# The fold of the last input piece on GpSimd, and its two hidden-transform blocks right behind the routing list

## The chip, the cores and the metric

The kernel runs on one core of a Trainium2 chip. The metric is the device time of one execution in microseconds (us). Five engines work side by side, each through its own instructions in order: TensorE (PE, with its weight loads as PEld), VectorE (DVE), ScalarE (ACT), GpSimd (POOL) and SyncE (SP, which issues DMAs).

## The reference

```
x = A_x                                   # 1 x 2048 x 448, float32
g = sigmoid((x * gate_w).sum(-1))
a = Real(DFT_seq(DFT_hidden(x)))          # both DFTs as products with the given cos and sin matrices
b = mixture of experts on x:              # 8 experts, F = 1792, top 2 of softmax(x @ wg)
      h = gelu(x @ w1[e]);  y = h @ w2[e];  b = sum of the two experts, weighted
out = g * a + (1 - g) * b
```

## The kernel before, in words

The first 40 us or so hold the DFT branch and the routing. The experts, a long chain of matmuls on TensorE, follow.

**The DFT branch.** The input comes in four pieces `c` = 0 to 3 of 512 rows each, tile `xraw` (`XR[c]`), each by two DMAs of 512 KB, one for each half `r`. The symmetries of the DFT are folded in with additions and subtractions: `fold_near` (line 501, `pq` from `xraw`), `fold_half` (505 and 506, `eo` from `pq`), `fold_quarter` (518, `fr` from `eo`). Each instruction here has 512 elements on 128 partitions, or 1024 for `fold_near` where both halves go together, and both inputs lie in SBUF. `pq` and `eo` have two buffers each, so piece 3 uses those of piece 1. A folded piece gives two blocks `v` = 2c and 2c+1. `hidden(v)` (line 527) multiplies `fr` of a block by the hidden DFT's matrix and ACT copies the result to `ab[:, v]` (line 528). `even(m)` then uses blocks 0 to 3 for the sequence DFT (line 466), `odd(m, v)` uses blocks 4 to 7 (line 570).

**The routing**, a generator stepped by `advance()`. The logits of all pieces end in a PSUM tile. DVE picks the two best experts of each token (252 to 265, up to tile `mb`), TensorE counts (269 to 275), and DVE makes two lists `oh` and `ov` (285 to 301), which TensorE joins with 16 small matmuls (309, the routing list's matmuls). From these come `tok0` (313), the rows that the first expert gathers. GpSimd issues these gathers (547, tiles `hi`, `lo`, `up`, `dn`, `xg`), and TensorE transposes each gathered tile (`turn0`, 683).

**Order.** Instructions of PE, DVE, ACT and SP run in the order in which the code is written (a manual schedule). GpSimd's queue is left to the scheduler. In the kernel before, GpSimd does constants in the first 4.4 us and then nothing until the first gather. Piece 3 is folded by DVE behind the routing list: half of `fold_near` before the first gather is issued, the rest behind `upper(0)` and `upper(1)`, which are ACT's preparation of the first expert weights. `hidden(6)` and `hidden(7)` follow all of `odd` for blocks 4 and 5, and `odd` for blocks 6 and 7 comes last.

Of the kernel before, what the change touches and what calls it, by code (L numbers as in the profile page):

```python
# [15 lines left out]
OP = mybir.AluOpType  # L16
# [31 lines left out]
NQT = QT // P  # L48
# [14 lines left out]
def r32(ap):  # L63
    return ap.bitcast(F32)
# [7 lines left out]
def tile_kernel(ctx: ExitStack, tc: tile.TileContext, xt, xrows, xplain, wg, whid, cq, cw, cspec, edge, refs, wquad, whall, cgen, wcat, out):  # L72
    nc = tc.nc
    te, ve, se, gp, sp = nc.tensor, nc.vector, nc.scalar, nc.gpsimd, nc.sync
# [16 lines left out]
    XR = {}  # L91
# [93 lines left out]
    def halves(acc):  # L185
        return acc.rearrange("p (u n) -> p u n", u=2)[:, :, :HE]
# [23 lines left out]
    def upper(k):  # L210
        W[k] = [stream.tile([P, DX], F32R, name=n) for n in ("hi", "lo")]
        V[k] = [stream.tile([P, DX], F32R, name=n, bufs=4) for n in ("up", "dn")]
        for (hi, _), raw in zip((W[k], V[k]), RAW[k]):
            se.activation(hi[:, : raw.shape[-1]], raw, AF.Copy)  # L214
# [255 lines left out]
    def advance(n=1):  # L470
        for _ in range(n):
            next(route, None)
# [4 lines left out]
    FH, LT, PQ, EO = {}, {}, {}, {}  # L477
# [18 lines left out]
    def fold_near(c, *rs):  # L496
        if c not in PQ:
            PQ[c] = hp.tile([P, 2, 2, 2, P], F32, name="pq")
            EO[c] = hp.tile([P, 2, 2, 2, P], F32, name="eo")
        for r in rs:  # L500
            ve.tensor_tensor(PQ[c][:, r], XR[c][:, r, :, 0], XR[c][:, r, :, 1], OP.add)

    def fold_half(c, r):
        raw, pq, eo = XR[c], PQ[c], EO[c]
        ve.tensor_tensor(eo[:, r, 0], pq[:, r, :, 0], pq[:, r, :, 1], OP.add)
        ve.tensor_tensor(eo[:, r, 1], pq[:, r, :, 0], pq[:, r, :, 1], OP.subtract)
        if c == 0:
            if r.start:
                ve.tensor_copy(xs, eo[:, 1, 0, :, 0:1].to_broadcast([P, 2, P]))
                for k in range(2):  # L510
                    ve.tensor_tensor(eo[:, k, 0, :, 0:1], raw[:, 0, :, 0, k, 0:1], raw[:, 0, :, 1, 1 - k, 0:1], OP.add)
                ve.memset(eo[:, 0, 1, :, 0:1], 0.0)

    def fold_quarter(c, *rs):
        if c not in FH:
            FH[c] = hp.tile([P, 2, 2, 2, P], F32, name="fr", bufs=NQT)
        for r in rs:
            ve.tensor_tensor(FH[c][:, r], EO[c][:, 0], EO[c][:, 1], OP.subtract if r else OP.add)

    def hidden(v, between=None):  # L520
        fr = FH[v // 2][:, v % 2]
        acc = ps.tile([P, 512], F32, name="acc")
        for u in range(2):
            if between and u == 1:
                between()
            for c in range(2):
                te.matmul(acc[:, 256 * u + HH * c : 256 * u + HH * (c + 1)], fr[:, u, c], wr[:, u, c], start=True, stop=True)
        se.activation(ab[:, v], halves(acc), AF.Copy)

    def special():  # L530
        acc = ps.tile([P, 512], F32, name="acc")
        for c in range(2):
            te.matmul(acc[:, HH * c : HH * (c + 1)], xs[:, c], wr[:, 0, c], start=True, stop=True)
        se.activation(mid[:, 1], acc[:, :HE], AF.Copy)
# [7 lines left out]
    def gather0(c, n):  # L542
        if c < FULL:
            XG[c] = r32(stream.tile([P, DX], F32R, name=("hi", "lo", "up", "dn")[c], bufs=3 if c < 2 else 4))
        else:
            XG[c] = xp.tile([P, NQ, P], F32, name="xg", bufs=2).rearrange("p q d -> p (q d)")
        gp.indirect_dma_start(out=XG[c][:n], out_offset=None, in_=xplain,
                              in_offset=bass.IndirectOffsetOnAxis(ap=rt["tok0"][:n, c : c + 1], axis=0))
# [34 lines left out]
    for r in range(2):  # L583
        fold_near(0, r)
        fold_half(0, slice(r, r + 1))
    fold_quarter(0, 0, 1)
    logits(0, 0)
    turn_over(3)
# [5 lines left out]
    hidden(0)  # L594
    hidden(1)
    fold_near(1, slice(0, 2))
    fold_half(1, slice(0, 2))
    fold_quarter(1, 0, 1)
    logits(2, 0, 1)
    evacuate(2)  # L600
# [6 lines left out]
    hidden(3)  # L607
    flip(3)
    fold_near(2, slice(0, 2))
    fold_half(2, slice(0, 2))  # L610
    fold_quarter(2, 0)
    se.activation(ch[:, :, 0:1], spec[:, 3:, None], AF.Copy)
    special()
    even(0)
# [7 lines left out]
        fetch(k)  # L622
    even(3)
    hidden(4)
    fold_near(3, 0)
    hidden(5)
    odd(0, 4)
    advance(2)
    for c, n in enumerate(tl0[:FULL]):
        gather0(c, n)  # L630
    advance()
    for v in (4, 5):
        for m in range(v == 4, NQT):
            odd(m, v)
    upper(0)
    upper(1)
    fold_near(3, 1)
    fold_half(3, slice(0, 2))
    fold_quarter(3, 0, 1)
    hidden(6)  # L640
    hidden(7)
    hid_stack.close()

    xp = ctx.enter_context(tc.tile_pool(name="xp", bufs=2))
# [530 lines left out]
    hidden = dram.tile([NT, P, 2 * D], F32, name="hidden")  # L1175
# [140 lines left out]
```

## Time and profile before

| | us |
|---|---|
| median of 3 runs | 633.23 |
| lowest and highest run | 633.11, 633.78 |
| the profiled execution | 633.83 |
| its span, first to last instruction | 632.0 |
| PE busy in the span | 622.2 (98%) |
| DVE busy | 506.0 (80%) |
| ACT busy | 289.3 (46%) |
| POOL busy | 214.7 (34%) |

The profiled execution is 0.60 us over the median, and 1.83 us of it lie outside its span. Busy shares are averages over very different stages: PE is busy nearly everywhere, so a microsecond counts if PE waits in it.

### The profile page before, as it was taken

What the parts mean: (1) busy time and instruction counts of PE and PEld (TensorE: products, weight loads), DVE (VectorE), ACT (ScalarE), POOL (GpSimd) and SP (SyncE); (2) the same over time, 40 slices, a digit from 0 to 9 for tenths busy, and PEclk for the clock granted to TensorE, in tenths of its full rate; (3) what the DMA queues carried; (4) which work ended last, traced back from release to release, by engine and by line L of the source; (5) the groups of instructions that cost most, each with busy time, mean ns of one, the idle gap of its engine ahead of it and who ended that gap; (6) DMA issues with size and microseconds to landing.
All of it is one profiled execution on the core that took longest, in us unless ns stands there. A gap on an engine that the chain in (4) does not pass through costs nothing. (4 is left out here: it accounts for less than half of the span.)

```text
span 632.0 us, 10936 instructions
## 1 busy us (share of the span) xinstructions
PE 622.2 (98%) x3581; PEld 556.6 (88%) x3581; DVE 506.0 (80%) x1262; ACT 289.3 (46%) x588; POOL 214.7 (34%) x198
## 2 busy tenths in 40 slices
PE   9999999999999999999999999999999999999995
PEld 5999999999998999989999788888888888888884
DVE  8889798679977999779896799988997788665561
ACT  2553233555565566564664434333342334544440
POOL 2210074635154353344450444333341342142113
PEclk9999999999999999999999999999999999999998
DMA  8556454597777777776776867879576637768734
GB/s 343 183 155 214 146 192 145 159 257 231 219 223 196 200 241 233 222 185 210 243 236 209 204 187 241 261 195 287 176 220 193 152 119 150 158 157 159 154 68 60
DMA packets 58751, 122.97 MB, mean 195 GB/s; under 512 B 8304, under 2 KB 31920, under 8 KB 58688
## 3 DMA queue, kind: packets, MB, share of 16 engines
q1 hardware_dynamic: 47376, 101.95, 50.0%
q0 software_dynamic: 11168, 20.20, 17.9%
q8 instruction: 30, 0.49, 0.3%
q14 instruction: 33, 0.27, 0.1%
q10 hardware_dynamic: 144, 0.07, 0.0%
HBM read 106.09 MB, written 16.08 MB: 193 GB/s over the span
## 5 line engine op out<-in xcount | busy, mean ns | idle before, releaser
L766 PE MATMUL acc<-X,hi 128*128 128x288 f32 (+3 forms) x1050 | 216.1, 342 | 0.0
L653 POOL DMA_INDIRECT xg<-xrows,piece x115 | 126.3, 1098 | 212.2 <-DVE xq L662 130.9
L766 PEld LDWEIGHTS acc<-X,hi 128*128 128x128 f32 x1050 | 173.8, 188 | 19.6 <-issue 1.4
L826 PE MATMUL y<-up,gh 128*128 128x448 f32 (+1 forms) x458 | 167.4, 366 | 0.0
L826 PE MATMUL y<-dn,gh 128*128 128x448 f32 (+1 forms) x458 | 167.4, 366 | 0.0
L826 PE MATMUL y<-up,gl 128*128 128x448 f32 (+1 forms) x444 | 162.5, 366 | 0.0
L773 ACT ACTIVATE g<-acc 128x288 f32<-128x288 f32 (+3 forms) x126 | 61.8, 491 | 194.6 <-issue 106.5
L766 PE MATMUL acc<-X,lo 128*128 128x288 f32 (+3 forms) x672 | 134.8, 322 | 0.0
L766 PEld LDWEIGHTS acc<-X,lo 128*128 128x128 f32 x672 | 105.6, 188 | 10.2
L889 POOL DMA_INDIRECT out<-ys,tok x36 | 63.8, 1771 | 110.9 <-DVE ys L877 53.3
L826 PEld LDWEIGHTS y<-up,gh 128*128 128x128 f32 (+1 forms) x458 | 85.8, 187 | 7.6
L826 PEld LDWEIGHTS y<-dn,gh 128*128 128x128 f32 (+1 forms) x458 | 85.8, 187 | 7.6
L790 DVE TENSOR_TENSOR gl<-g,gh 128x512 fp32r<-128x512 f32 (+1 forms) x111 | 76.4, 689 | 19.5 <-ACT gh L784 13.3
L930 DVE CUSTOM_DVE_ANT_0 junk<-quads 128x512 f32<-128x512 f32 x128 | 88.0, 687 | 2.2
L826 PEld LDWEIGHTS y<-up,gl 128*128 128x128 f32 (+1 forms) x444 | 83.2, 187 | 7.3 <-DVE gl L790 0.2
L219 DVE TENSOR_TENSOR lo<-raw,hi 128x512 fp32r<-128x512 f32 x112 | 77.0, 687 | 2.0 <-ACT hi L214 1.1
L786 DVE CAST gh<-g 128x512 fp32r<-128x512 f32 (+2 forms) x69 | 30.5, 441 | 57.1 <-ACT g L773 56.8
L214 ACT ACTIVATE hi<-raw 128x512 fp32r<-128x512 f32 x112 | 69.4, 619 | 0.0
L219 DVE TENSOR_TENSOR dn<-row,up 128x448 fp32r<-128x448 f32 x112 | 69.1, 617 | 0.0
L214 ACT ACTIVATE up<-row 128x448 fp32r<-128x448 f32 x112 | 63.3, 565 | 0.4 <-DMA row<-wcat 0.4
L771 ACT ACTIVATE g<-acc 128x256 f32<-128x256 f32 x42 | 16.1, 383 | 48.2 <-PE acc L766 47.9
L773 ACT ACTIVATE g<-g 128x256 f32<-128x256 f32 x42 | 17.6, 418 | 37.4 <-DVE g L772 37.4
(276 smaller groups left out, 435.2 us busy)
## 6 DMA issues: line engine op xcount, KB each, us to landing
quads<-cq SPq DMA_DIRECT2D x64, 512.0 KB, 5.2
raw<-wcat SPq DMA_DIRECT2D x112, 256.0 KB, 2.9
row<-wcat SPq DMA_DIRECT2D x112, 224.0 KB, 3.4
out<-yt SPq DMA_DIRECT2D x21, 224.0 KB, 3.2
xraw<-xt SPq DMA_DIRECT2D x8, 512.0 KB, 6.9
out<-ot POOLq DMA_DIRECT2D x16, 224.0 KB, 4.0
cw<-cw SPq DMA_DIRECT2D x4, 512.0 KB, 9.3
xg<-xrows,piece POOLq DMA_INDIRECT x115, 3.7
```

Of the source, the lines that this page charges most:

```text
L214: se.activation(hi[:, : raw.shape[-1]], raw, AF.Copy)
L219: ve.tensor_tensor(lo[:, :n], raw, r32(hi[:, :n]), OP.subtract)
L653: st = gp.indirect_dma_start(out=xg[:, q], out_offset=None, in_=xrows, in_offset=bass.IndirectOffsetOnAxis(ap=rt["piece"][:, e, g : g + 1] ...
L766: te.matmul(acc[:, :m], a, b, start=s == 0, stop=s == len(steps) - 1)
L771: se.activation(g[:, cs], acc[:, n : 2 * n], AF.Copy)
L773: se.activation(g[:, cs], g[:, cs] if both else acc[:, :n], AF.Gelu_apprx_tanh)
L786: ve.tensor_copy(gh[:, :top], g[:, :top])
L790: ve.tensor_tensor(gl[:, :main], g[:, :main], r32(gh[:, :main]), OP.subtract)
L826: te.matmul(Y[c][:m, :D], a, b, start=f == 0 and s == 0, stop=f == NF - 1 and s == len(steps) - 1)
L889: st = gp.indirect_dma_start(out=out, out_offset=bass.IndirectOffsetOnAxis(ap=rt["tok"][:n, e, c : c + 1], axis=0), in_=ys[:n], in_offset= ...
L930: ve.tensor_tensor_reduce(out=junk[:, :512], in0=row(a[0])[:, a[1] * 512 : a[1] * 512 + 512], in1=row(b[0])[:, b[1] * 512 : b[1] * 512 + 5 ...
```

## The change

Everything is the same but for piece 3. Its six fold instructions run on GpSimd, written right behind the fold of piece 2. `hidden(6)` and `hidden(7)` are written behind the gathers' issue, ahead of `odd` for blocks 4 and 5.

```diff
     def fold_near(c, *rs):
         for r in rs:
-            ve.tensor_tensor(PQ[c][:, r], XR[c][:, r, :, 0], XR[c][:, r, :, 1], OP.add)
+            (gp if c == NQT - 1 else ve).tensor_tensor(PQ[c][:, r], XR[c][:, r, :, 0], XR[c][:, r, :, 1], OP.add)
     def fold_half(c, r):
-        ve.tensor_tensor(eo[:, r, 0], pq[:, r, :, 0], pq[:, r, :, 1], OP.add)
-        ve.tensor_tensor(eo[:, r, 1], pq[:, r, :, 0], pq[:, r, :, 1], OP.subtract)
+        by_c = gp if c == NQT - 1 else ve
+        by_c.tensor_tensor(eo[:, r, 0], pq[:, r, :, 0], pq[:, r, :, 1], OP.add)
+        by_c.tensor_tensor(eo[:, r, 1], pq[:, r, :, 0], pq[:, r, :, 1], OP.subtract)
     def fold_quarter(c, *rs):
         for r in rs:
-            ve.tensor_tensor(FH[c][:, r], EO[c][:, 0], EO[c][:, 1], OP.subtract if r else OP.add)
+            (gp if c == NQT - 1 else ve).tensor_tensor(FH[c][:, r], EO[c][:, 0], EO[c][:, 1], OP.subtract if r else OP.add)
...
     fold_quarter(2, 0)
+    fold_near(3, 0, 1)
+    fold_half(3, slice(0, 2))
+    fold_quarter(3, 0, 1)
...
     hidden(4)
-    fold_near(3, 0)
     hidden(5)
     odd(0, 4)
     advance(2)
     for c, n in enumerate(tl0[:FULL]):
         gather0(c, n)
+    hidden(6)
+    hidden(7)
     advance()
     for v in (4, 5):
         for m in range(v == 4, NQT):
             odd(m, v)
     upper(0)
     upper(1)
-    fold_near(3, 1)
-    fold_half(3, slice(0, 2))
-    fold_quarter(3, 0, 1)
-    hidden(6)
-    hidden(7)
```

PE, from the last of the routing list's matmuls, before (`y_...` are the PSUM tiles that collect `odd` of the four `m`):

```order
L309 MATMUL acc<-ov,oh 32x20
L570 MATMUL y_499<-ab,cw 128x226
L570 MATMUL y_501<-ab,cw 128x226
L570 MATMUL y_503<-ab,cw 128x226
L570 MATMUL y_460<-ab,cw 128x226
```

Three more of these follow, then the transform of blocks 6 and 7 (`x8`, the input `fr`), `odd` of block 6 and the first gathered tile's transposes:

```order
L527 MATMUL acc<-wr,fr 128x113 x8
L570 MATMUL y_460<-ab,cw 128x226
L570 MATMUL y_499<-ab,cw 128x226
L570 MATMUL y_501<-ab,cw 128x226
L570 MATMUL y_503<-ab,cw 128x226
L683 MATMUL acc<-ident,hi 128x128 x4
```

PE at the same place in the changed kernel (lines are one higher, the tiles have other numbers):

```order
L309 MATMUL acc<-ov,oh 32x20
L528 MATMUL acc<-wr,fr 128x113 x8
L571 MATMUL y_517<-ab,cw 128x226
L571 MATMUL y_519<-ab,cw 128x226
L571 MATMUL y_521<-ab,cw 128x226
L571 MATMUL y_466<-ab,cw 128x226
```

The two blocks now stand directly behind the list, and all eleven `odd` instructions run behind them without a break in the order.

DVE behind the routing's lists, as the difference (`-` before, `+` changed). `pq`, `eo` and `fr` are the fold's tiles:

```order
 L301 TENSOR_TENSOR ov<-og,tokid 128x320
-L501 TENSOR_TENSOR pq<-xraw 128x512
 L304 TENSOR_SCALAR dz<-y_195 128x16
-L305 TENSOR_TENSOR dz<-m_350,mx 128x16
-L313 CAST tok_482<-acc 32x5 x2
-L501 TENSOR_TENSOR pq<-xraw 128x512
-L505 TENSOR_TENSOR eo<-pq 128x2x256
-L506 TENSOR_TENSOR eo<-pq 128x2x256
-L518 TENSOR_TENSOR fr<-eo 128x512 x2
+L305 TENSOR_TENSOR dz<-m_359,mx 128x16
+L313 CAST tok_488<-acc 32x5 x2
```

The six fold instructions are gone from DVE, and nothing else moved there.

GpSimd (POOL) in the changed kernel, from its last constant to the second gather. Before, the gathers stand directly behind `ahead_of`:

```order
L145 AFFINE_SELECT ahead_of<-same 128x136
L501 TENSOR_TENSOR pq<-xraw 128x512 x2
L506 TENSOR_TENSOR eo<-pq 128x2x256
L507 TENSOR_TENSOR eo<-pq 128x2x256
L519 TENSOR_TENSOR fr<-eo 128x512 x2
L548 DMA hi<-xplain,tok_488 128x512
L548 DMA lo<-xplain,tok_488 128x512
```

The fold is the only work on GpSimd between its constants and the gathers.

## Rows read from the trace of the kernel before

**Rows 1.** TensorE in order of time. Columns: start and length in us, engine, line, operation, output<-input, shape, count (a float32 matmul of the code counts as two), and in brackets the idle time before and what ended it.

```profile
1.37 4.02 PE L117 MATMUL y<-warm 128*128 128x512 bf16 x9 [1.37 <-DVE warm L112]
...
6.83 0.82 PE L117 MATMUL y<-warm 128*128 128x512 bf16 x3
...
17.03 4.00 PE L466 MATMUL acc<-ab,cw 128*128 128x226 f32 x20
20.86 0.22 PE L269 MATMUL y<-ones,mb 128*128 128x128 bf16 x1
...
23.49 1.94 PE L527 MATMUL acc<-wr,fr 128*128 128x113 f32 x16
25.26 0.56 PE L570 MATMUL y<-ab,cw 128*128 128x226 f32 x2
25.84 0.56 PE L309 MATMUL acc<-ov,oh 128*32 128x20 f16 x16
26.33 2.94 PE L570 MATMUL y<-ab,cw 128*128 128x226 f32 x14
29.70 2.01 PE L527 MATMUL acc<-wr,fr 128*128 128x113 f32 x16 [0.43 <-DVE fr L518]
31.93 1.80 PE L570 MATMUL y<-ab,cw 128*128 128x226 f32 x8 [0.22 <-ACT ab L528]
33.57 0.60 PE L683 MATMUL acc<-ident,hi 128*128 128x128 f32 x4
```

**Rows 2.** Busy time of each engine in the expert stage, then the granted TensorE clock as a share of full speed, the DMA share and the GB/s.

```profile
60.00:620.00 560.00, 560.00 (x3095) 503.12 (x3095) 452.91 (x1104) 264.59 (x535) 200.75 (x165) 1.00 0.69 194
```

**Rows 3.** VectorE in order of time, columns as in Rows 1.

```profile
12.21 1.29 DVE L518 TENSOR_TENSOR fr<-eo 128x512 f32<-128x512 f32 x2
13.42 1.22 DVE L501 TENSOR_TENSOR pq<-xraw 128x1024 f32<-128x1024 f32 x1
...
16.00 0.69 DVE L518 TENSOR_TENSOR fr<-eo 128x512 f32<-128x512 f32 x1
16.79 0.29 DVE L252 TENSOR_REDUCE mx<-y 128x16 f32<-128x128 f32 x1
...
17.45 0.29 DVE L254 TENSOR_TENSOR key<-key,rev 128x128 f32<-128x128 f32 x1
...
18.09 0.29 DVE L256 TENSOR_TENSOR o<-key,k 128x128 f32<-128x128 f32 x1
...
20.36 0.29 DVE L265 TENSOR_TENSOR mb<-o,o 128x128 bf16<-128x128 f32 x1
...
25.30 0.49 DVE L301 TENSOR_TENSOR ov<-og,tokid 128x320 f16<-128x320 f32 x1
...
28.87 1.29 DVE L518 TENSOR_TENSOR fr<-eo 128x512 f32<-128x512 f32 x2
```

**Rows 4.** ScalarE in order of time: the activation table's load and the copies of blocks 6 and 7.

```profile
27.45 1.28 ACT L318 ACT_TABLE_LOAD   x1
...
31.35 0.97 ACT L528 ACTIVATE ab<-acc 128x452 f32<-128x452 f32 x2
```

**Rows 5.** The two DMAs of piece 3: their issue on SP in order of time, then, from the view of DMA issues of a stretch that holds one of them each (first, second), count, size and us from issue to landing. The last row is the same view's for the first gather.

```profile
5.27 0.82 SPq L103 DMA_DIRECT2D xraw<-xt  x2
...
xraw<-xt SPq DMA_DIRECT2D x1, 512.0 KB, 7.9
...
xraw<-xt SPq DMA_DIRECT2D x1, 512.0 KB, 8.8
...
hi<-xplain,tok POOLq DMA_INDIRECT x1, 4.9
```

**Rows 6.** GpSimd in order of time: a one-element constant, a 128-element instruction with one input, the last constants, gathers.

```profile
0.42 0.10 POOL L1304 MEMSET const-float32-0.0<- 128x1 f32 x1 [0.42 <-issue]
...
1.56 0.28 POOL masks.py:199 TENSOR_SCALAR_AFFINE_SELECT ident<-ident 128x128 f32<-128x128 f32 x1
...
3.63 0.23 POOL L475 MEMSET ch<- 128x128 f32 x1
...
27.77 1.52 POOL L547 DMA_INDIRECT hi<-xplain,tok  x1 [23.39 <-DVE pq L501]
...
33.03 0.94 POOL L547 DMA_INDIRECT dn<-xplain,tok  x1 [0.30 <-issue]
...
84.04 2.07 POOL L653 DMA_INDIRECT xg<-xrows,piece  x1 [0.30 <-DVE left L408]
...
89.07 2.23 POOL L653 DMA_INDIRECT xg<-xrows,piece  x1 [0.30 <-issue]
```

**Rows 7.** VectorE at the same times: two like instructions, one beside GpSimd's constants and one with GpSimd idle, and what ran during the last two rows of Rows 6.

```profile
2.71 1.18 DVE L143 TENSOR_SCALAR same<-ids,pe 128x8 bf16<-128x8 f32 x1
...
22.58 0.23 DVE L287 TENSOR_SCALAR top<-rkey,most 128x8 f32<-128x8 f32 x1
...
83.80 2.89 DVE L412 TENSOR_TENSOR vw<-ob,part 128x1280 bf16<-128x1280 f32 x2
...
89.00 1.48 DVE L412 TENSOR_TENSOR vw<-ob,part 128x1280 bf16<-128x1280 f32 x1
```

**Rows 8.** All of one line's VectorE instructions with two SBUF inputs over the span: ns minimum/median/maximum, first and last start in us.

```profile
L219 DVE TENSOR_TENSOR lo<-raw,hi x112: 669/685/762, 30.1 to 611.5; 128x512 fp32r<-128x512 f32 x112
```

## The prediction

> **What bounds the kernel now.** [...] What is in play is the time at which TensorE gets through the opening, and I read it in order of time for TensorE, then for DVE.
>
> TensorE shows two waits around piece 3 [rows 1]. The first block of piece 3 starts at 29.70 and waits for DVE's `fr`, which is being made from 28.87 on [rows 3]. At 31.93 `odd` of block 6 waits for ACT's copy of the same piece, which ran from 31.35 [rows 4]. Their real size comes from starts, since a matmul's end overlaps the next one. Eight `odd` instructions take 33.57 - 31.93 = 1.64, or 0.205 each, and the sixteen of a piece's transform 25.26 - 23.49 = 1.77. So the fourteen from 26.33 are through at 29.20, 0.50 before 29.70, and the transform from 29.70 is through at 31.47, 0.46 before 31.93. Two waits, 0.96 us together.
>
> The second thing to see is what TensorE waits for further ahead. The matmul at line 269 starts at 20.86 and needs DVE's `mb`, done at 20.36 + 0.29 = 20.65. The routing list's matmuls start at 25.84 and need `ov`, done at 25.30 + 0.49 = 25.79 [rows 1, 3]. DVE's chain from the fold of piece 2 through the routing is therefore as critical as TensorE: what delays it by more than 0.2 us stops TensorE.
>
> **The change, part by part.**
>
> *The two blocks moved ahead.* If piece 3 is folded by the end of the list's matmuls (26.33), blocks 6 and 7 run at once, ACT copies them under the fourteen `odd` matmuls (2.87 us), and both waits go: -0.96. ACT's table load of 1.28 and the weights' preparation come behind these copies instead of ahead of them. The copies end some 2 us after 26.33 and the rest ends where `ab`'s copies ended before, so ACT is free for the first transposed tile as before; no term. The first gathered tile has to be there when TensorE wants it: it landed at 27.77 + 4.9 = 32.7, and the change wants it at 33.57 - 0.96 = 32.6 [rows 1, 5, 6]. The gather itself gets faster. It took 1.52 with DVE folding beside it, and 0.94 for a like one at 33.03 with DVE idle, so it lands about half a microsecond earlier; no term.
>
> *The six instructions leave DVE.* They ran behind the list and their cover was TensorE's `odd` work; what they held up is in the 0.96.
>
> *The six instructions on GpSimd.* None of this kind is in the trace, so I bound one. GpSimd's 128-element instruction with one input took 0.28 and a one-element one 0.10 [rows 6], or 1.4 ns per element. 512 elements make 0.10 + 0.73 = 0.83 if two inputs cost no more than one, and 0.10 + 1.46 = 1.56 if they are read in turn. I take the middle, 1.19. [...]
>
> They can start when the data is there, 5.27 + 7.9 = 13.2 for the first half and 5.64 + 8.8 = 14.4 for the second (the second of the two issues is some 0.37 later) [rows 5]. Undisturbed, five more behind 14.4 end at 20.4, six microseconds before TensorE asks. Their own length costs nothing.
>
> *What they do to DVE.* This term decides. From 12.21 to 25.79 DVE is full, mostly with instructions that read two inputs from SBUF [rows 3]. The trace shows that such an instruction and GpSimd do not run freely beside each other. The gather at 84.04 took 2.07 against 0.94 for a free one. It began while the first of two `vw` products (two inputs in SBUF, about 1.4 each) was running, and the extra 1.13 is what was left of that product. The one at 89.07 took 2.23, and the product that began at 89.00 explains its extra 1.29 in the same way [rows 6, 7]. The reverse is there once. DVE's tiny instruction at 2.71 took 1.18, against 0.23 for its like at 22.58, and ended at 3.89, just as GpSimd's row of constants ended at 3.86. So each side can shut the other out for a whole instruction.
>
> [...]
>
> Worked out with turns taken: whoever waits gets the next turn. `fr` of piece 1 ends at 13.43; GpSimd's first add runs to 14.62; DVE's `pq` of piece 2 (1.22) to 15.84; GpSimd to 17.03; DVE's first `eo` (0.61, the pitch of the two `fr` in 1.29) to 17.64; GpSimd to 18.83; the second `eo` to 19.44; GpSimd to 20.63; `fr` (0.69) to 21.32; GpSimd's fifth to 22.51, under which DVE's first two routing instructions run, which have one input in PSUM. The third, `key` times `rev`, runs from 22.51 to 22.84, GpSimd's sixth to 24.03, and `o`, which started at 18.09 before, starts at 24.03. All of the routing behind it is late by 5.94. With 0.83 an instruction, the same walk gives 3.8, and with 1.56 it gives 8.1.
>
> If DVE wins each time both ask, GpSimd first gets in under `mx`, and then one-input instructions cover part of each of its six: 2.7, 3.6 or 5.4 for the three lengths. If GpSimd never lets go, as the row at 2.71 suggests, it is 6.9 for 1.19 an instruction. I take the turns.
>
> *The sum,* against the profiled execution: 633.83 - 0.96 + 5.94 = 638.8. The profiled execution is 0.6 over the median, so 638.2 for the median. Queued behind the late lists are the list's matmuls, `tok0`, the gathers and SP's first weight loads, all late by the same amount, so nothing is added.
>
> **The rivals.**
>
> *TensorE's clock falls in the new gap.* TensorE would stand from 20.86 to about 26.8. The first nine matmuls of the execution, after 1.37 of idling, stand some 0.42 apart; three of the same shape at 6.83 stand 0.22 apart [rows 1]. [...] Against it: no gap of this length stands in the trace behind the start, so nothing shows that one is long enough.
>
> *GpSimd does not slow DVE.* Then only the -0.96 stays: 632.3. It speaks for it that a line of 112 DVE instructions with two SBUF inputs, many beside gathers, has a median of 685 ns and a maximum of 762 [rows 8]: a gather hardly delays DVE. Against it: a gather reads a few indices, while these six read 512 elements twice. This is the case on the other side, and it decides where DVE's delay stays below 0.96.
>
> *DVE has the first turn:* 633.23 - 0.96 + 3.6 = 635.9. *GpSimd holds on:* 633.23 - 0.96 + 6.9 = 639.2.
>
> *Nothing changes:* the fold is late on GpSimd too, and blocks 6 and 7 wait again. That needs more than (26.33 - 14.4) / 5 = 2.4 an instruction, twice my value; with the lists late it needs more still. I give it no chance of its own.
>
> **How the numbers follow.** Turns with the clock kept, 0.33 (638.2); turns with the clock falling, 0.17 (640.7); DVE first, 0.17 (635.9); GpSimd holding on, 0.13 (639.2); no slowing, 0.20 (632.3). The likeliest is 638.2, and its own range, by the two lengths of an instruction, is 636.1 to 640.4. The whole range goes from 632.2 to 641.0 and leaves out the longest instruction with GpSimd holding on and falls of the clock on top of it. A change of 0.2% (1.27 us) is about what a measurement of this kernel can tell from none. The case without slowing gains 0.96 and lies within it; faster needs more than both waits, 0.03. The same is 0.17, slower 0.80.
>
> **What would show it.** Right: GpSimd's six instructions between 13 and 24 us; DVE's `pq`, `eo` and `fr` of piece 2 with durations over 1 us instead of 0.6 to 0.7, or gaps between them; `mb` done near 26.6 and `ov` near 31.7; TensorE idle before line 269 for about 6 us, and no wait ahead of blocks 6 and 7 or of `odd` of block 6. Wrong: `mb` still near 20.65. Then the lists' matmuls start at 25.84 and the first gathered tile's transposes near 32.6. If the transposes come no earlier than 33.57 although the two waits are gone, the gather is the new limit.

## The result, and the profile after

The changed kernel is slower: 639.1 us median of 6 runs (638.37 to 639.85) against 633.33 us of the kernel before (6 runs, 633.11 to 633.78). The ratio is 1.009 with a 95% interval of 1.0077 to 1.0103. The profiled execution took 639.84, its span is 638.0.

TensorE of the changed kernel in order of time, to be read against [rows 1] (start and length in us, engine, line, operation, tiles, count, idle time before and what ended it):

```profile
17.14 4.00 PE L466 MATMUL acc<-ab,cw 128*128 128x226 f32 x20
25.70 0.29 PE L269 MATMUL y<-ones,mb 128*128 128x128 bf16 x1 [4.56 <-DVE mb L265]
...
27.73 3.32 PE L466 MATMUL acc<-ab,cw 128*128 128x226 f32 x8
30.84 2.25 PE L528 MATMUL acc<-wr,fr 128*128 128x113 f32 x16
32.93 0.56 PE L571 MATMUL y<-ab,cw 128*128 128x226 f32 x2
33.42 0.56 PE L309 MATMUL acc<-ov,oh 128*32 128x20 f16 x16
33.91 2.04 PE L528 MATMUL acc<-wr,fr 128*128 128x113 f32 x16
35.79 4.38 PE L571 MATMUL y<-ab,cw 128*128 128x226 f32 x22
40.01 0.60 PE L683 MATMUL acc<-ident,hi 128*128 128x128 f32 x4
```

Three distances between starts hold the whole story. From the first of the twenty matmuls at line 466 to line 269 it is 25.70 - 17.14 = 8.56 instead of 20.86 - 17.03 = 3.83: +4.73, a wait for `mb`. From line 269 to the routing list's matmuls it is 33.42 - 25.70 = 7.72 instead of 4.98: +2.74. From there to the first transposes it is 40.01 - 33.42 = 6.59 instead of 7.73: -1.14, and neither of the two old waits is left. The sum is +6.33; the span grew by 6.0.

VectorE, for [rows 3]:

```profile
13.51 2.29 DVE L501 TENSOR_TENSOR pq<-xraw 128x1024 f32<-128x1024 f32 x1
15.83 1.64 DVE L506 TENSOR_TENSOR eo<-pq 128x512 f32<-128x512 f32 x1
17.40 1.75 DVE L507 TENSOR_TENSOR eo<-pq 128x512 f32<-128x512 f32 x1
19.19 1.64 DVE L519 TENSOR_TENSOR fr<-eo 128x512 f32<-128x512 f32 x1
...
21.07 0.29 DVE L253 TENSOR_TENSOR key<-y,mx 128x128 f32<-128x128 f32 x1
21.39 0.71 DVE L254 TENSOR_TENSOR key<-key,rev 128x128 f32<-128x128 f32 x1
22.14 0.29 DVE L255 TENSOR_REDUCE k<-key 128x16 f32<-128x128 f32 x1
22.46 0.92 DVE L256 TENSOR_TENSOR o<-key,k 128x128 f32<-128x128 f32 x1
...
25.35 0.29 DVE L265 TENSOR_TENSOR mb<-o,o 128x128 bf16<-128x128 f32 x1
...
28.04 0.17 DVE L285 SCALAR_TENSOR_TENSOR rkey<-y,rev 128x8 f32<-128x8 f32 x1 [1.80 <-PE y L275]
...
31.16 0.49 DVE L301 TENSOR_TENSOR ov<-og,tokid 128x320 f16<-128x320 f32 x1
```

GpSimd, for [rows 6]:

```profile
13.40 3.53 POOL L501 TENSOR_TENSOR pq<-xraw 128x512 f32<-128x512 f32 x2 [9.01 <-DMA xraw<-xt]
17.00 1.60 POOL L506 TENSOR_TENSOR eo<-pq 128x512 f32<-128x512 f32 x1
18.57 1.72 POOL L507 TENSOR_TENSOR eo<-pq 128x512 f32<-128x512 f32 x1
20.36 2.86 POOL L519 TENSOR_TENSOR fr<-eo 128x512 f32<-128x512 f32 x2
35.32 1.19 POOL L548 DMA_INDIRECT hi<-xplain,tok  x1 [12.09 <-ACT tok L313]
```

Six VectorE instructions with two SBUF inputs carry the delay, one for each of GpSimd's six: `pq` 2.29 instead of 1.22, the two `eo` 1.64 and 1.75 and `fr` 1.64 instead of 0.69 each, `key` 0.71 and `o` 0.92 instead of 0.29. The excess is 1.07 + 0.95 + 1.06 + 0.95 + 0.42 + 0.63 = 5.08. Between them the instructions with one input in PSUM (line 253) and the reduction (line 255) kept their 0.29. `mb` was done at 25.64, 4.99 late.

Busy time by stretch, with the granted clock after POOL's column, for the gap and the two stretches behind it:

```profile
21.00:25.30 4.30, 0.14 (x1) 0.00 (x0) 3.96 (x12) 0.00 (x0) 2.22 (x2) 0.93 0.00 0
25.30:29.30 4.00, 3.60 (x12) 3.14 (x13) 2.04 (x10) 0.82 (x2) 0.00 (x0) 0.50 0.01 4
29.30:34.00 4.70, 4.70 (x40) 4.20 (x38) 2.25 (x10) 1.64 (x3) 0.00 (x0) 0.77 0.53 141
```

TensorE stood for 4.56 us, and the granted clock behind it is 0.50, and 0.77 over the next stretch, where [rows 2] and the opening of the kernel before have 1.00. VectorE's lists were not the limit there: `ov` was done at 31.65, 1.77 ahead of the list's matmuls, while eight matmuls at line 466 took 3.32 instead of 1.74.

### The profile page after: what moved, and what is told of

Same layout as the page of the kernel before. It is cut to its first block, busy times and chain, and to the rows that moved or that the text cites. A ratio compares the mean times of both kernels' runs of the same rounds, so it can differ in the third digit from the quotient of the medians.

```text
span 638.0 us, 10935 instructions
## 1 busy us (share of the span) xinstructions
PE 624.1 (98%) x3581; PEld 558.6 (88%) x3581; DVE 507.3 (80%) x1256; ACT 289.2 (45%) x588; POOL 223.5 (35%) x204
```

## The experiments

The theory: a GpSimd instruction that reads SBUF and a VectorE instruction with two SBUF inputs shut each other out, so GpSimd's adds take VectorE's time nearly one for one on a chain without slack, and the gap that this opens on TensorE also costs its clock. Rivals: the fold's own dependencies or the moved blocks make the delay; any GpSimd work does; the second loss is no matter of the clock.

All runs are read by the same three distances on TensorE, from the first matmul at line 466 to line 269 (A), on to the routing list's matmuls (B), on to the first transposes (C):

| run | A | B | C | median, us | ratio to before (95%) |
|---|---|---|---|---|---|
| before | 3.83 | 4.98 | 7.73 | 633.0 to 633.3 | |
| changed | 8.56 | 7.72 | 6.59 | 639.1 | 1.009 (1.0077 to 1.0103) |
| e1_own_adds | 8.41 | 6.41 | 7.23 | 639.65 | 1.0107 (1.0091 to 1.0124) |
| e2_writes_only | 3.84 | 4.99 | 8.08 | 633.82 | 1.0013 (1.0002 to 1.0023) |
| e3_fold_on_dve | 6.88 | 6.43 | 6.59 | 637.35 | 1.0075 (1.0058 to 1.0091) |
| e4_keep_warm | 8.15 | 4.98 | 6.64 | 637.41 | 1.0068 (1.0052 to 1.0085) |
| e5_blocks_back | 8.38 | 6.58 | 7.17 | 639.01 | 1.0097 (1.0081 to 1.0112) |
| e6_one_on_gp | 4.39 | 5.00 | 7.31 | 633.61 | 1.0013 (1.0003 to 1.0022) |
| e7_dve_gap | 3.89 | 4.98 | 6.93 | 632.42 | 0.9991 (0.9982 to 1.0) |
| e8_copy_order | 3.89 | 4.98 | 7.26 | 633.01 | 0.9998 (0.9989 to 1.0007) |
| e9_one_input | 4.90 | 4.99 | 7.60 | 634.64 | 1.0029 (1.0017 to 1.004) |
| e10_gap_and_list | 3.83 | 4.99 | 7.03 | 632.56 | 0.999 (0.9981 to 0.9999) |

From the first transposes to the end of the span it is 597.8 to 598.8 us in all twelve profiles, so what tells these kernels apart lies in the opening, and differences below 1 us between two single profiles are not to be read from their spans.

### Six adds that nobody needs, in the kernel before (e1_own_adds)

```diff
     fold_quarter(2, 0)
+    scr = hp.tile([P, 2, 2, P], F32, name="scr", bufs=1)
+    for i in range(6):
+        gp.tensor_tensor(scr, XR[3][:, i % 2, :, 0], XR[3][:, i % 2, :, 1], OP.add)
     se.activation(ch[:, :, 0:1], spec[:, 3:, None], AF.Copy)
```

> The kernel before, with piece 3 folded by VectorE in its old place, and six two-input adds of 128x512 on GpSimd that read piece 3 and write a tile that nobody reads, where the changed kernel has its fold. The shared-access theory (a GpSimd instruction that reads SBUF and a VectorE instruction with two SBUF inputs exclude each other) expects VectorE's fold of piece 2 stretched as in the changed kernel, the tile mb done near 25.6 us instead of 20.65, TensorE's clock at half after the gap, and no gain: 633.3 + 4.8 for the gap + 2.7 for the clock = 640 to 641. The rival, that the delay in the changed kernel comes from the fold's own dependencies (buffers, semaphores between the two engines, the moved blocks), expects mb at 20.65 and 633.3.

VectorE's fold of piece 2 and TensorE's wait in this run:

```profile
12.91 2.29 DVE L501 TENSOR_TENSOR pq<-xraw 128x1024 f32<-128x1024 f32 x1
15.23 1.64 DVE L505 TENSOR_TENSOR eo<-pq 128x512 f32<-128x512 f32 x1
16.80 1.76 DVE L506 TENSOR_TENSOR eo<-pq 128x512 f32<-128x512 f32 x1
18.59 1.64 DVE L518 TENSOR_TENSOR fr<-eo 128x512 f32<-128x512 f32 x1
```

```profile
25.16 0.29 PE L269 MATMUL y<-ones,mb 128*128 128x128 bf16 x1 [4.35 <-DVE mb L265]
```

The four durations are those of the changed kernel to 0.01, with the fold left on VectorE, no block moved and no result of GpSimd used by anyone. So dependencies and moved blocks are out; the work beside VectorE makes the delay. This run has the loss and, of the gain, only 0.50 in distance C: the wait for `fr` is still there (0.41 by the row), while the one for ScalarE's copy is gone although nobody moved it (more on this at e8). Its median is the highest of all, but its executions (639.23 to 640.29) overlap with those of the changed kernel. It is 0.35 below the expected 640; in the profile B grew by 1.43 and not by 2.7.

### Work on GpSimd that only writes (e2_writes_only)

```diff
     fold_quarter(2, 0)
+    scr = hp.tile([P, 2, 2, P], F32, name="scr", bufs=1)
+    gp.tensor_copy(scr[:, 0, 0, :1], XR[3][:, 0, 0, 0, 0, :1])
+    gp.tensor_copy(scr[:, 0, 0, 1:2], XR[3][:, 1, 0, 0, 0, :1])
+    for i in range(12):
+        gp.memset(scr, 0.0)
```

> The kernel before, with twelve memsets of 128x512 on GpSimd at the same place, after two one-element copies that wait for piece 3; some 6 us of GpSimd work that writes and reads nothing. If only GpSimd's reads exclude VectorE's two-input instructions, mb stays at 20.7 and the time within 0.5 us of 633.3. If any GpSimd instruction does (as VectorE's 1.18 us instruction at 2.71 beside GpSimd's constants suggests), mb is late by 3 to 6 us and the time is 636 to 641.

GpSimd's memsets, and VectorE beside them:

```profile
14.31 6.93 POOL L616 MEMSET scr<- 128x512 f32 x12
```

```profile
14.24 0.69 DVE L505 TENSOR_TENSOR eo<-pq 128x512 f32<-128x512 f32 x1
14.86 0.68 DVE L506 TENSOR_TENSOR eo<-pq 128x512 f32<-128x512 f32 x1
```

6.93 us of memsets cost VectorE nothing in any instruction that ran beside them, and distances A and B are those of the kernel before. So it is GpSimd's reading that counts here for instructions with two SBUF inputs. The median is 0.8 us over the kernel before all the same, more than the 0.5 that was expected. In the profile, 0.35 of that stands in distance C, where TensorE waited 0.57 instead of 0.22 for ScalarE's copy, which stood behind a weight DMA that landed later (ScalarE waited 0.58 for it instead of 0.41); the rest stays open.

### The fold at the new place, but on VectorE (e3_fold_on_dve)

```diff
-            (gp if c == NQT - 1 else ve).tensor_tensor(PQ[c][:, r], ...)
+            ve.tensor_tensor(PQ[c][:, r], ...)
...
-        by_c = gp if c == NQT - 1 else ve
+        by_c = ve
```

(and the same in `fold_quarter`.)

> The changed kernel with the six fold instructions back on VectorE, in the changed order: they stand on VectorE between the fold of piece 2 and the routing. Their own length there is 0.61 x 4 + 1.29 = 3.7 us, so mb comes at 24.3 instead of 25.64 on GpSimd, and TensorE's gap is 3.5 instead of 4.6 us. The theory that GpSimd takes VectorE's time one for one and more expects it faster than the changed kernel: 633.3 + 3.5 - 1.1 = 635.7 with the clock kept, up to 638.4 if it falls. The rival, that GpSimd at least hides part of the fold, expects it slower than the changed kernel, over 639.1.

TensorE's wait for `mb`:

```profile
23.94 0.29 PE L269 MATMUL y<-ones,mb 128*128 128x128 bf16 x1 [2.89 <-DVE mb L265]
```

and the busy times with the granted clock in a stretch behind it:

```profile
25.30:29.30 4.00, 4.00 (x24) 3.69 (x23) 2.63 (x11) 1.20 (x3) 0.00 (x0) 0.77 0.02 4
```

VectorE does the six in 3.9 us (16.18 to 20.04), and A is 6.88; GpSimd's six made it 8.56. Moving the fold to the second engine cost more of VectorE's time (5.08) than VectorE needs for the fold itself. The median is 1.75 us below that of the changed kernel, but the intervals of the two ratios overlap, so the reading rests on A. Against the sum with the clock kept (635.7) the median is 1.65 higher; B is 6.43 instead of 4.98 and the granted clock 0.77, so the clock fell behind this gap of 2.89 too, for a shorter stretch.

### The gap filled with matmuls (e4_keep_warm)

```diff
-    even(2, advance)
+    even(2, lambda: (turn_over(20), advance()))
```

> The changed kernel with twenty more matmuls of 128x512 that no result uses, put on TensorE right ahead of the matmul that waits for mb, so that some 4.3 us of the 4.6 us gap are filled. mb and the start of line 269 stay near 25.7. The theory that 2.7 us of the loss are TensorE at half clock behind the gap expects a granted clock of 1.00 there, the routing list's matmuls near 30.7 instead of 33.42, and 639.1 - 2.7 = 636.4. The rival, that these 2.7 us come from waits or from VectorE, expects 639.1 or more.

TensorE, and the granted clock behind the place of the gap:

```profile
20.98 4.48 PE L117 MATMUL y<-warm 128*128 128x512 bf16 x20
25.30 0.22 PE L269 MATMUL y<-ones,mb 128*128 128x128 bf16 x1
...
30.28 0.56 PE L309 MATMUL acc<-ov,oh 128*32 128x20 f16 x16
```

```profile
25.30:29.30 4.00, 4.00 (x30) 3.90 (x29) 2.30 (x11) 1.67 (x4) 0.00 (x0) 1.00 0.00 0
```

Line 269 starts within 0.4 of the changed kernel, the clock stays at 1.00, and B is 4.98 again, to the hundredth. So the 2.74 us by which B had grown in the changed kernel's profile are the clock. Line 269 waited for the filling matmuls here: `mb` was done at 24.36. The time fell by 1.7 in the median, not by the 2.7 that was expected. The granted clock averaged over a whole execution is 0.996 in all four of this run, as in the kernel before (0.996 to 0.998), but 0.992 to 0.995 in the six of the changed kernel, with 0.992 and 0.993 in the three longest, the profiled one among them. What the clock costs thus differs from one execution to the next; other profiles with a fall show 1.43 (e1), 1.45 (e3) and 1.60 (e5) in B, with 0.63, 0.77 and 0.57 granted from 25.3 to 29.3 where the changed kernel has 0.50.

This run shows something else in its first row on VectorE. Here `pq` of piece 2 started ahead of GpSimd's first add (12.91 against 13.44) and kept its 1.22:

```profile
12.91 1.22 DVE L501 TENSOR_TENSOR pq<-xraw 128x1024 f32<-128x1024 f32 x1
14.16 1.65 DVE L506 TENSOR_TENSOR eo<-pq 128x512 f32<-128x512 f32 x1
```

In the changed kernel it started at 13.51, behind GpSimd's 13.40, and took 2.29. GpSimd was ahead in the same way, by 0.18, 0.12 and 0.11, and `pq` took 2.29, in e1, e5 and e6. In these five runs the engine that started first went first, and where more than one add ran they then took turns.

### The blocks back in their place (e5_blocks_back)

```diff
-    hidden(6)
-    hidden(7)
     advance()
...
     upper(1)
+    hidden(6)
+    hidden(7)
```

> The changed kernel with blocks 6 and 7 back in their old place, behind odd of block 5 and behind the first experts' weights; the fold stays on GpSimd. mb, the gap and the clock stay as in the changed kernel. If the two waits of 0.50 and 0.46 us were the gain of the move, one of them (for fr) is gone by the early fold alone and the other (for ACT's copy of the block) comes back: up to 0.5 us slower than the changed kernel, 639.1 to 639.6. If the blocks' move has a hand in the loss, it is faster than 638.4.

C is 7.17: with the early fold the first wait is gone without the move (7.73 - 7.17 = 0.56), the second is back (0.34 of idling by its row, 0.50 by the starts), and the move is worth the rest, 0.58. The medians (639.01 and 639.1) can't tell it, since the clock's cost varies by more.

### One of the six on GpSimd (e6_one_on_gp)

```diff
-            ve.tensor_tensor(PQ[c][:, r], ...)
+            (gp if c == NQT - 1 and r == 0 else ve).tensor_tensor(PQ[c][:, r], ...)
...
     fold_quarter(2, 0)
+    fold_near(3, 0)
...
-    fold_near(3, 0)
```

> The kernel before with one of the six fold instructions (the first near add) on GpSimd behind the fold of piece 2, the other five on VectorE in their old places. Price by instruction: VectorE's pq of piece 2 waits for it once and takes 2.29 instead of 1.22 us, mb comes 1.1 later, near 21.75, TensorE's gap is under 1 us and the clock stays up. The fold behind the list is one instruction shorter, which takes up to 0.5 from the first wait: 633.0 + 0.9 - 0.5 = 633.4, and the routing list's matmuls near 26.7. A fixed cost of using GpSimd at all would show as 3 us or more.

The add on GpSimd, and VectorE beside it:

```profile
12.86 1.31 POOL L501 TENSOR_TENSOR pq<-xraw 128x512 f32<-128x512 f32 x1 [8.48 <-DMA xraw<-xt]
```

```profile
11.76 1.29 DVE L518 TENSOR_TENSOR fr<-eo 128x512 f32<-128x512 f32 x2
12.97 2.29 DVE L501 TENSOR_TENSOR pq<-xraw 128x1024 f32<-128x1024 f32 x1
```

One add costs VectorE 1.07, the same as the first in the changed kernel, so there is no price for using GpSimd at all beyond that of the instruction. A grew by 0.56 only. Of the 1.07, some 0.2 fell into time in which VectorE would have waited for TensorE's last logits, and some 0.3 into the time by which `mb` is ready before TensorE asks (without GpSimd, in e7, `mb` is done at 20.24 and line 269 starts at 20.60). TensorE's wait was 0.34, and the clock stayed (1.00 behind it, B 5.00).

The median was 633.61, as forecast within 0.2, but partly by luck. `mb` was done at 21.08 instead of 21.75, and C shrank by 0.42 at another place than forecast: the wait for `fr` is still 0.48, and the one for ScalarE's copy is gone.

### Copies instead of adds (e9_one_input)

```diff
-        gp.tensor_tensor(scr, XR[3][:, i % 2, :, 0], XR[3][:, i % 2, :, 1], OP.add)
+        gp.tensor_copy(scr, XR[3][:, i % 2, :, 0])
```

(from the first experiment's kernel)

> The kernel before, with six copies of 128x512 on GpSimd (one SBUF input each) at the place where the six two-input adds stood in the run with own adds; nothing else differs between the two. If any read of SBUF by GpSimd shuts out VectorE's two-input instructions for the copy's whole length, VectorE's fold of piece 2 is stretched again, each of its instructions by a copy of 0.5 to 0.8 us instead of 1.1; mb comes 2 to 3.5 us late and the time is 635 to 638. If two reads at once on GpSimd are needed for that, mb stays at 20.7 and the time near 633.0.

GpSimd's first copy, and VectorE beside it:

```profile
13.15 0.76 POOL L614 COPY scr<-xraw 128x512 f32<-128x512 f32 x1 [8.77 <-DMA xraw<-xt]
```

```profile
12.15 1.29 DVE L518 TENSOR_TENSOR fr<-eo 128x512 f32<-128x512 f32 x2
13.37 1.63 DVE L501 TENSOR_TENSOR pq<-xraw 128x1024 f32<-128x1024 f32 x1
15.03 0.98 DVE L505 TENSOR_TENSOR eo<-pq 128x512 f32<-128x512 f32 x1
15.94 1.09 DVE L506 TENSOR_TENSOR eo<-pq 128x512 f32<-128x512 f32 x1
```

One input is enough to hold VectorE up, but for less: 0.41, 0.29 and 0.40 in these three instructions and up to 0.44 in a later one, where an add holds it for 0.95 to 1.07. A is 4.90, the gap 0.91, the clock stays (1.00 behind it, B 4.99), and the time of 634.64 is 0.4 under the forecast's lower end.

These rows on GpSimd seem to hold its own waiting too. The copy started at 13.15, while VectorE's `fr` ran until 13.44; what is left behind that is 0.47, and `pq` was held up for 0.41. The add of e6 started at 12.86, with `fr` until 13.05; what is left is 1.12, and `pq` was held up for 1.07. So a copy costs less because it is shorter, not because it shuts VectorE out for less of its length. If `pq` waited out GpSimd's whole instruction in both runs, these two rows agree to 0.06 us; in the later turns the hold is shorter by up to some 0.2, for adds and copies alike.

### The same two waits taken away without GpSimd (e7_dve_gap)

```diff
     fold_quarter(2, 1)
+    fold_near(3, 0)
...
     hidden(4)
-    fold_near(3, 0)
+    fold_near(3, 1)
...
     upper(0)
-    upper(1)
-    fold_near(3, 1)
     fold_half(3, slice(0, 2))
     fold_quarter(3, 0, 1)
     hidden(6)
+    upper(1)
     hidden(7)
```

> No GpSimd. The kernel before with the first near add of piece 3 put into VectorE's gap of 0.93 us in the routing (while it waits for line 275), the second one where the first stood, and on ScalarE the copies of blocks 6 and 7 put ahead of and behind the second expert weights' preparation instead of behind both. mb and the routing list's matmuls stay at 20.7 and 25.8, fr is ready by 28.8, and both waits go: 633.0 - 0.96 = 632.1, faster than both kernels. If the first gathered tile is what TensorE then waits for, its transposes stay near 33.5 and the time at 633.0.

```profile
28.85 1.94 PE L527 MATMUL acc<-wr,fr 128*128 128x113 f32 x16
30.62 1.71 PE L570 MATMUL y<-ab,cw 128*128 128x226 f32 x8
32.51 0.63 PE L683 MATMUL acc<-ident,hi 128*128 128x128 f32 x4 [0.18 <-DMA hi<-xplain,tok]
```

A and B are unchanged, both waits are gone, and C is 6.93, a gain of 0.80. A third wait of 0.18 takes some of it: the first gather now lands last. The median is 0.6 us under the kernel before, with the interval ending at 1.0, so it is the lowest of all, but the times alone do not show a gain; the distances do, in one profile.

ScalarE's order alone (e8_copy_order):

```diff
     upper(0)
-    upper(1)
     fold_near(3, 1)
     fold_half(3, slice(0, 2))
     fold_quarter(3, 0, 1)
     hidden(6)
+    upper(1)
     hidden(7)
```

> The kernel before with only ScalarE's order changed: the copies of blocks 6 and 7 ahead of and behind the second expert weights' preparation. The wait for fr (0.50) stays, the wait for the copy (0.46) goes: 633.0 - 0.46 = 632.5, half of what the kernel with the fold moved as well gains. If the late weights hold VectorE up instead, 633.0 or more.

C is 7.26, 0.47 shorter, as expected of the one wait; the median does not show it (0.9998, 0.9989 to 1.0007). There is a reason to doubt that every execution of the kernel before has this wait. In its profile ScalarE stood 0.41 us for a weight DMA just ahead of the two copies:

```profile
30.87 0.58 ACT L214 ACTIVATE up<-row 128x448 fp32r<-128x448 f32 x1 [0.41 <-DMA row<-wcat]
```

In e6, with ScalarE's order untouched, it did not stand there (the same instruction starts at 30.63, at the pitch of the one before), and in e1 and e6 TensorE did not wait for the copy (C of 7.23 and 7.31); in e2 it stood 0.58, and TensorE stood longer too, 0.57. So the 0.46 depends on when a weight lands, and how much of it a usual execution has is not known.

And, on top of e7, all four pieces of `tok0` copied by VectorE (e10_gap_and_list):

```diff
-            (ve.tensor_copy if q < 2 else se.copy)(tok0[r], ...)
+            ve.tensor_copy(tok0[r], ...)
```

> The kernel with the near adds of piece 3 in VectorE's gap and the copies' order on ScalarE, and in addition all four pieces of tok0 copied by VectorE, where ScalarE's two waited for VectorE's two. In the kernel without this step TensorE's transposes still waited 0.18 us for the first gather, and stood 6.93 behind the list's matmuls where 6.59 is what the work takes. With tok0 ready some 0.2 earlier the gather lands earlier and the distance is 6.6 to 6.75: 632.42 - 0.25 = 632.2, and 0.8 us faster than the kernel before. If VectorE's two more copies hold up fr by 0.3, the wait is only exchanged and the time stays at 632.4.

C is 7.03 instead of 6.93 and the median 632.56 instead of 632.42: no better. VectorE's `fr` came later by the two copies (it starts 2.64 behind the list's matmuls instead of 2.30), and the wait was exchanged, as the second half of the expectation said.

## Why the prediction was right, point by point

**The two waits.** The sum had -0.96; the profile has -1.14 in distance C and no wait at either block. The missing 0.18 lies in how the waits were sized: where nothing holds them up, the fourteen `odd` matmuls take 2.78 (26.07 to 28.85 in e7) and not 2.87, and the eight behind the second wait take 1.54 (in e8) and not 1.64. That second wait was taken as fixed; e1 and e6 do without it, and e2 and e6 show that it hangs on a weight DMA. The gather did get faster, with 1.19 for the first one where [rows 6] have 1.52, and 3.5 us from its issue to its landing where [rows 5] have 4.9.

**The deciding step.** That GpSimd's adds and VectorE's two-input instructions shut each other out was read from three rows [rows 6, 7] and is shown by the first experiment. The turns came as walked through: `pq`, `eo`, `eo` and `fr` each once behind an add, the fifth and sixth partly covered by instructions with at most one SBUF input, which kept their 0.29. The size was off. An add was put at 1.19; it is 1.12 long once VectorE's own instruction has ended (e6), its hold on VectorE is 0.95 to 1.07, and the last two held `key` and `o` for only 0.42 and 0.63. So `mb` was late by 4.99, not by 5.94.

One of the three rows was read too widely. The 1.18 us instruction beside GpSimd's constants is another kind of VectorE instruction, and the constants beside it write only, but for `tri` (2.65, 0.30 long), which reads `ones`; the second experiment shows that writing does not hold up two-input ones. What held that instruction is not shown.

**The clock.** The likeliest case kept it, and it fell. "No gap of this length stands in the trace behind the start" was said against it, and that was the step that failed: behind the gap of 4.56 us the granted clock was 0.50 and then 0.77, worth 2.74 in the profiled execution. The case with the fall had been put at 640.7 with half the chance of the other. No run shows the 2.5 us by which that lies over 638.2, an upper bound of the author's; in its place the runs show 2.74, 1.43, 1.45 and 1.60 in B (the changed kernel, e1, e3, e5). The slow pace of the first nine matmuls, 0.42 apart instead of 0.22, goes with a granted clock that reads 1.00 over the first 5 us; no run shows that this slow start and the fall behind a gap are the same thing.

**The sum.** -0.96 + 5.94 = +4.98 was forecast, and the profile has 4.73 + 2.74 - 1.14 = +6.33. In the median it is 638.2 against 639.1, inside the range. The delay was 1.2 us too large as a term (4.73 against 5.94; 0.2 of it is the slack that the prediction had itself found ahead of line 269 and left out of its sum), and the clock's 1.4 to 2.7 was not in it. The two went against each other, so it is luck that the number is better than its terms. It is the same with `ov`: it was done at 31.65, near the 31.7 that was named, because `mb` came about 1 us earlier than forecast and VectorE, which the prediction had called full there, stood 1.80 instead of 0.93 for line 275 on the slower TensorE.

**The rivals.** GpSimd not slowing VectorE (632.3) is out by the result and by e1. VectorE having the first turn each time, and GpSimd never letting go, are both out by the alternation in the rows; who begins depends on who starts first, and that differed between the changed kernel's profile and that of e4.

## What to carry to other kernels

Before work goes from VectorE to GpSimd, look at what VectorE runs beside it: in these runs two-input instructions on SBUF and GpSimd's adds and copies that read SBUF took turns, with 0.95 to 1.07 us of VectorE's time for a full turn behind an add of 512 elements and 0.29 to 0.44 for one behind a copy. On a chain without slack the move can so cost more than the work itself, here 8.56 against 6.88 us in distance A. GpSimd work that only writes (6.93 us of memsets in e2) went side by side with them, and so did VectorE work with one input in PSUM and reductions with GpSimd's adds (0.28 to 0.29 us, as before). And a wait on TensorE is to be priced with what the clock does behind it: here 2.89 us of standing cost 1.45 more in B (e3), while 0.91 us cost nothing (e9); what lies between was not tried.

## What had not been expected of the hardware

The clock's cost behind gaps of much the same length differs: 2.74 us in B behind 4.56, but 1.43 (e1) and 1.60 (e5) behind 4.35 and 4.32, and mean clocks of 0.992 to 0.995 over six executions of the changed kernel. A GpSimd copy of 512 elements held VectorE's instructions up for only 0.29 to 0.44 us, an add for 0.95 to 1.07, close to the 0.47 and 1.12 that they last once VectorE's own instruction has ended. And twelve memsets of 128x512 on GpSimd, 6.93 us of work, did not lengthen a single VectorE instruction beside them.
